# Another order for the start of a fused attention and gated-MLP kernel, with two attention visits and two weight steps moved

## The chip, the cores and the metric

One core of a Trainium2 chip runs the whole program. The time is that of one execution on the device, in microseconds (us). TensorE (PE in the profile) multiplies matrices, VectorE (DVE) and ScalarE (ACT) work on vectors, GpSimd (POOL) does elementwise work too, and the queues of SyncE (SP), ACT and POOL issue the transfers.

## The reference

```
scores = scale * np.matmul(q, k.transpose(0, 1, 3, 2))        # q, k, v: 8 x 8 heads x 576 x 64, fp32
masks = np.stack([mask_plain if h < H // 2 else mask_dil for h in range(H)])   # window 32, or 32 at every 4th key
attn = np.exp(scores - max); attn = attn / (sum + 1e-09)
x = (attn @ v).transpose(0, 2, 1, 3).reshape(B * S, H * D)    # 4608 tokens x 512
g = x @ w_gate                                                # 512 x 1536
out = (g * (1 / (1 + exp(-g))) * (x @ w_val)) @ w_out         # 1536 x 512
```

## The kernel before

**Tokens and packs.** The 4608 tokens are 12 chunks of 384. The attention of a chunk is four packs (two heads each), numbered on through the chunks. A pack's life is a row of steps: Q scores (L320 puts the mask, L326 the products), S subtracts the row maximum (L340, L341 on DVE), X is the exponential (L346 on ACT), T turns the exponentials on TensorE (L350), K copies them out of PSUM (L356 on ACT), A multiplies by the values (L366), N divides by the sums (L375 to L377 on DVE), U turns the result (L384), H and L make the two halves of x (L413 on ACT, L417 on DVE). Chunk 0's four packs are all worked at the start of the program; the later packs are worked between the matrix products of the MLP.

**Products in two halves.** Every fp32 operand is a sum of a high part, rounded to fp32r, and a low part, and a product is three matmuls: high x high, high x low, low x high. In the first four chunks a step s of `for s in range(NS)` is one block of 128 hidden columns: 12 matmuls for the gate (`gv_mm(ci, f, 0)`, bank bg, L428), 12 for the value (bank bv, L428), and 12 of the step before for the output (`out_mm`, banks bo, L465). Between them ACT makes the tanh (L437), DVE multiplies the gate in place (`dve_u`, L442) and the value (`dve_h`, L447), ACT and POOL split h in two halves (L452, L457). The gate's bank is single: the next gate products wait for L442.

**Weights.** They arrive as raw 64-bit words and each unit (half a block; block f has units 2f and 2f+1) goes through five steps, which the table of the start names W0 to W4: W0 the exponents (E, L207 on ACT), W1 a shift (T: L225 on ACT for units 1, 2 and odd ones from 5 on, else L228 on DVE), W2 the join of the two words (B: L235 or L238 on DVE), W3 the high half (H, L246 on ACT), W4 the low half (L, L250 on POOL). Every token `Wn` takes the next unit that has not had that step. A raw buffer is loaded again when step B of its unit is done.

**What sets the order.** During the start the list of tokens is the order in which TensorE, DVE and ACT get the instructions. After it a scheduler places the instructions; the program's calls (`w_upto`, `attend`) give it their order. `visits(m, a, b)` says in which of the slots (three to a step s) pack m's first visit A (scores of m, results of m-1) and second visit B (turning of both) are written.

Of the kernel before, what the change touches and what calls it, by code (L numbers as in the profile page):

```python
# [106 lines left out]
def attention_moe(ctx, tc, qkb, vb, w, masks, ident, out):  # L107
# [148 lines left out]
    def w_upto(**to):  # L256
        for c, n in to.items():
            while done[c] < min(n, NU):
                w_one(c)

    def w_one(c):
        u = done[c]
        done[c] += 1
        if c == "E":
            w_exp(u)
        elif c == "T":
            w_shift(u)
        elif c == "B":
            w_bits(u)
            while ready["w"] and w_load():  # L270
                pass
        elif c == "H":
            w_split_hi(u)
        else:
            w_split_lo(u)
# [145 lines left out]
    def gv_mm(ci, f, which):  # L421
        bank = (bank_g, bank_v)[which]
        xh, xl = x_hi[ci % 2], x_lo[ci % 2]

        ops = [(j, 0, x) for j in range(NK) for x in (xh, xl)] + [(j, 1, xh) for j in range(NK)]
        for n, (j, low, x) in enumerate(ops):
            o = 4 * P * (j // 2) + 2 * P * which + P * (j % 2)
            nc.tensor.matmul(out=bank[:, :CH], lhsT=wcol(f, o, low), rhs=x[ORDER[j]],  # L428
                             start=n == 0, stop=n == len(ops) - 1)
# [5 lines left out]
    def act_tanh(i):  # L435
        t = t_ring()
        nc.scalar.activation(out=t, in_=bank_g[:, :CH], func=AF.Tanh, scale=0.5)  # L437
        hst[i] = [t, None, None]

    def dve_u(i):  # L440
        t = hst[i][0]
        last["h"] = nc.vector.scalar_tensor_tensor(out=t, in0=t, scalar=1.0, in1=bank_g[:, :CH],  # L442
                                                   op0=ALU.add, op1=ALU.mult)

    def dve_h(i):
        t = hst[i][0]
        last["h"] = nc.vector.scalar_tensor_tensor(out=t, in0=t, scalar=0.5, in1=bank_v[:, :CH],  # L447
                                                   op0=ALU.mult, op1=ALU.mult)

    def h_hi(i):  # L450
        hh = hh_ring(dt=F32R)
        nc.scalar.copy(out=hh, in_=hst[i][0])  # L452
        hst[i][1] = hh

    def h_lo(i):
        hl = at(M_H + 4 * CH, CH, F32R)
        nc.gpsimd.tensor_tensor(out=hl, in0=hst[i][0], in1=hst[i][1], op=ALU.subtract)  # L457
        hst[i][2] = hl

    def out_mm(i):  # L460
        f = i % NF
        _, hh, hl = hst.pop(i)

        for j, low, x in [(j, low, hh) for j in range(4) for low in range(2)] + [(j, 0, hl) for j in range(4)]:
            nc.tensor.matmul(out=bank_o[j][:, :CH], lhsT=wcol(f, 2 * DM + P * j, low), rhs=x,  # L465
                             start=f == 0 and low == 0 and x is hh, stop=f == NF - 1 and x is hl)

    def out_store(ci):
        for j in range(4):
            ot = at(M_RAW + 8 * WU - CH * (j + 1), CH)  # L470
            if j % 2 == 0:
                nc.scalar.copy(out=ot, in_=bank_o[j][:, :CH])
            else:
                nc.vector.tensor_copy(out=ot, in_=bank_o[j][:, :CH])
            nc.sync.dma_start(out=out[P * j:P * j + P, CH * ci:CH * ci + CH], in_=ot)
# [47 lines left out]

    et = mybir.EngineType
    with tc.manual_schedule(engines={et.PE, et.DVE, et.Activation}):
        for what in ("Q0 Q1 S0 X0 T0 S1 K0 X1 A0 M0 W0 Q2 N0 T1 K1 S2 X2 Q3 W1 S3 X3 A1 U0 N1 W2 T2 K2 H0 L0 W0 W3 "
                     "W4 T3 A2 K3 W1 U1 N2 A3 H1 L1 W0 W2 U2 N3 W3 H2 U3 L2 W4 H3 L3 W1 W0 W2 W1 W2 W3 W0 W0").split():
            first[what[0]](int(what[1]))
    ab.close()
    bank_g, bank_v, two, *bank_o = [bank(ctx, *x) for x in (("bg", 1), ("bv", 1), ("two", 2), ("bo0", 1), ("bo1", 1),  # L530
# [13 lines left out]
    def visits(m, a, b):  # L544
        visit[a], visit[b] = ("A", m), ("B", m)
# [1 line left out]

    M1 = 4 * NPLAIN + 8
    for n in range(5):
        visits(4 + n, 5 + 13 * n // 2, 8 + 13 * n // 2)  # L550
    for m in range(9, M1 - 12):
        visits(m, NB * m // 4 - NB - 6, NB * m // 4 - NB - 2)
    for n in range(13):
# [8 lines left out]
    def attend(now):  # L562
        what, m = visit.get(now, ("", 0))
        if what == "A":
            if m > 4:
                results(m - 1, two)
            if m < NPK:
                scores(m, two, m < 8)
            if m > 4:
                norm(m - 1, two, later)  # L570
            if m < NPK:
                shift(m, two, later, m < 8)
                exps(m)

                with tc.issue_after(last["e"].ins):
                    load_v(m, later, nc.scalar)
                if m + 1 < NPK:
                    load_qk(m + 1, later, nc.scalar)
        elif what == "B":
            if m > 4:  # L580
                turn_y(m - 1, two[:, 0])
            if m < NPK:
                turn_e(m, two[:, 1])
                keys(m, two[:, 1], later)
            if m > 4:
                x_copies(m - 1, two[:, 0])
# [81 lines left out]
    def ask(n):  # L668

        nonlocal asked  # L670
        while asked < min(n, NPIECE * NC):
            taken[asked] = at(M_RING + PIECE * (asked % NAT), PIECE, F32R)
            nc.gpsimd.dma_start(out=taken[asked], in_=pieces[asked % NPIECE])  # L673
            asked += 1
# [31 lines left out]
    def x_step(n, ci):  # L706
        b11, b12, b21, b22 = [x32[a][t] for a in range(2) for t in range(2)]
        if ci == 0:
            b11, b21 = x32_first
        x1 = x1_at[min(ci, 1)]  # L710
        steps = [lambda: x_split(0, b11), lambda: x_split(1, b21), lambda: tt(nc.vector, x1, b12, b11),
                 lambda: x_split(3, x1), lambda: tt(nc.vector, x1, b22, x1), lambda: x_split(2, x1),
                 lambda: tt(nc.vector, b12, b22, b12), lambda: tt(nc.vector, b21, b21, x1),
                 lambda: x_split(4, b12), lambda: x_split(5, b21), lambda: x_split(6, b22)]
        if n < len(steps):
            steps[n]()
# [66 lines left out]
    def n_out(ci, t, i):  # L783
        return NT * NP * ci + NP * t + i
# [9 lines left out]
    def mix_to(half):  # L794

        while mixed < half * 9 * NP // 62:
            mix_stage()

    for s in range(NS):
        ci, f = divmod(s, NF)  # L800
        W = 2 * s
        w_upto(L=W + 3)
        gv_mm(ci, f, 0)
        act_tanh(s)
        w_upto(H=W + 4, E=W + 6)
        attend(3 * s)
        dve_u(s)
        mix_to(2 * (s - NF) + 1)
        with tc.issue_after(last["h"].ins):
            w_upto(T=W + 5, B=W + 5)  # L810
        w_upto(L=W + 4, H=W + 5, E=W + 7)
        gv_mm(ci, f, 1)
        attend(3 * s + 1)
        dve_h(s)
        h_hi(s)
        with tc.issue_after(last["h"].ins):
            w_upto(T=W + 6, B=W + 6)
        if s > 0:
            out_mm(s - 1)
        h_lo(s)  # L820
        if s > 0 and f == 0:
            out_store(ci - 1)
        attend(3 * s + 2)

        mix_to(2 * (s - NF) + 2)
        if ci == NPLAIN - 1:
            if f >= 9:
                ask([4, 7, NAT - 1][f - 9])
            for n in {5: (0,), 6: (1,), 7: (2,), 8: (3,), 9: (4, 5), 10: (6, 7, 8), 11: (9, 10)}.get(f, ()):
                x_step(n, 0)  # L830


    for ci in range(NC):
# [14 lines left out]
        for t in range(NT):  # L848
            for i in range(NP):
                n = n_out(ci, t, i)  # L850
# [60 lines left out]
```

## Time and profile before

| | us |
|---|---|
| median of 3 runs | 955.54 (955.46 to 956.37) |
| the profiled execution, its own time | 955.79 |
| its span, first to last instruction | 953.8 |

| engine | busy us | share of the span |
|---|---|---|
| TensorE matmul | 940.8 | 99% |
| TensorE weight load | 915.3 | 96% |
| DVE | 658.4 | 69% |
| ACT | 406.9 | 43% |
| POOL | 378.8 | 40% |

The busy share is a mean over the whole program. The change touches its first hundred us alone, so what counts is which engine waits there, and for what.

### The profile page before, as it was taken

To read this page: it belongs to the slowest core of one execution; us is meant where nothing else is said; L and a number is where in the kernel's file an instruction comes from. 1 tells how busy PE (TensorE), PEld (TensorE's weight loads), DVE (VectorE), ACT (ScalarE), POOL (GpSimd) and SP (SyncE) were. 2 spreads that over 40 slices of the span, in tenths; PEclk is the share of its full clock that TensorE was granted. 3 is DMA by queue.
4 is the path that set the end of the run, shared out by engine and by line. 5 is a ranking of instruction groups with operands and counts; after the bars stand their busy time and mean duration, and the time that the engine had idled before them with its cause. 6 is when DMAs were issued, how large, how long until landed. Compare 5 with 4: busy or idle time off the path is not lost.

```text
span 953.8 us, 23938 instructions
## 1 busy us (share of the span) xinstructions
PE 940.8 (99%) x9960; PEld 915.3 (96%) x9960; DVE 658.4 (69%) x1168; ACT 406.9 (43%) x788; POOL 378.8 (40%) x460
## 2 busy tenths in 40 slices
PE   7899999999999999999999999999999999999998
PEld 5898999999999999999999999999999999999998
DVE  4966557667767654776887677789487779466583
ACT  4885332333234323444554344446234446234352
POOL 0865421111112222344276334465244448354472
PEclk9999999999999999999999999999999999999999
DMA  9976154666766781989888998889988878988883
GB/s 367 344 260 202 35 205 160 228 208 220 241 231 224 253 308 56 288 262 297 269 263 278 339 288 259 264 251 298 350 264 283 254 236 267 317 250 255 252 238 121
DMA packets 86060, 238.12 MB, mean 250 GB/s; under 512 B 8768, under 2 KB 29120, under 8 KB 85952
## 3 DMA queue, kind: packets, MB, share of 16 engines
q0 software_dynamic: 36288, 132.14, 44.9%
q1 hardware_dynamic: 36848, 65.07, 19.5%
q10 hardware_dynamic: 12816, 39.38, 12.3%
q8 instruction: 79, 1.29, 0.6%
q14 instruction: 29, 0.24, 0.1%
HBM read 194.08 MB, written 42.47 MB: 248 GB/s over the span
## 4 chain that ended last, share of the span: by engine, by line
PE 89%; DVE 6%; ACT 3%; issue 1%; DMA 1%; POOL 0%; ACTq 0%; DVEq 0%; POOLq 0%; SPq 0%
PE bo L741 31%; PE bg L741 11%; PE bv L741 11%; PE bo L465 9%; PE bv L428 9%; PE bg L428 9%; PE two L366 3%; PE two L326 2%; PE two L350 2%; PE two L384 1%; DVE at_float32r L700 1%; DVE at_int L235 1%; ACT at_int L207 1%; DVE at_int L238 1%; ACT at_int L225 1%
## 5 line engine op out<-in xcount | busy, mean ns | idle before, releaser
L741 PE MATMUL bo<-at_float32r,at_float32r 128*128 128x384 f32 x1728 | 318.8, 336 | 0.0
L741 PEld LDWEIGHTS bo<-at_float32r,at_float32r 128*128 128x128 f32 x1728 | 299.9, 188 | 1.1
L673 POOL DMA_DIRECT2D at_float32r<-pieces x252 | 137.8, 547 | 245.5 <-PE bo L741 141.6
L700 DVE TENSOR_TENSOR at_float<-bo,at_float 128x384 f32<-128x384 f32 x224 | 122.3, 554 | 101.5 <-PE bo L741 51.9
L457 POOL TENSOR_TENSOR at_float32r<-at_float,at_float32r 128x384 fp32r<-128x384 f32 x48 | 57.3, 1193 | 215.7 <-PE bo L465 179.7
L741 PE MATMUL bg<-at_float32r,at_float32r 128*128 128x384 f32 x648 | 137.1, 337 | 0.0
L741 PE MATMUL bv<-at_float32r,at_float32r 128*128 128x384 f32 x648 | 136.6, 336 | 0.0
L741 PEld LDWEIGHTS bv<-at_float32r,at_float32r 128*128 128x128 f32 x648 | 114.2, 188 | 0.5
L741 PEld LDWEIGHTS bg<-at_float32r,at_float32r 128*128 128x128 f32 x648 | 113.8, 188 | 0.7
L700 DVE TENSOR_TENSOR at_float32r<-at_float,at_float32r 128x384 fp32r<-128x384 f32 (+1 forms) x112 | 101.5, 930 | 18.3 <-ACT at_float32r L730 14.3
L428 PE MATMUL bg<-at_float32r,at_float32r 128*128 128x384 f32 x576 | 111.6, 340 | 1.4 <-POOL at_float32r L250 0.8
L428 PE MATMUL bv<-at_float32r,at_float32r 128*128 128x384 f32 x576 | 111.3, 340 | 0.0
L730 ACT CAST at_float32r<-at_float 128x384 fp32r<-128x384 f32 x168 | 82.6, 512 | 65.2 <-PE bv L741 21.9
L465 PE MATMUL bo<-at_float32r,at_float32r 128*128 128x384 f32 x576 | 109.3, 337 | 0.0
L700 POOL TENSOR_TENSOR at_float32r<-at_float,at_float32r 128x384 fp32r<-128x384 f32 x84 | 91.6, 1091 | 43.9 <-ACT at_float32r L730 42.8
L428 PEld LDWEIGHTS bg<-at_float32r,at_float32r 128*128 128x128 f32 x576 | 100.4, 188 | 3.0 <-POOL at_float32r L250 1.1
L428 PEld LDWEIGHTS bv<-at_float32r,at_float32r 128*128 128x128 f32 x576 | 100.4, 188 | 0.9
L465 PEld LDWEIGHTS bo<-at_float32r,at_float32r 128*128 128x128 f32 x576 | 100.6, 188 | 0.4
L767 ACT ACTIVATE at_float<-at_float 128x384 f32<-128x384 f32 x96 | 50.6, 527 | 99.6 <-DVE at_float L700 99.6
L442 DVE SCALAR_TENSOR_TENSOR at_float<-at_float,bg 128x384 f32<-128x384 f32 x48 | 26.6, 553 | 73.3 <-ACT at_float L437 73.3
L746 ACT COPY at_float<-bg 128x384 f32<-128x384 f32 x84 | 40.3, 479 | 82.3 <-PE bg L741 82.1
L700 DVE TENSOR_TENSOR at_float<-at_float,at_float 128x384 f32<-128x384 f32 (+1 forms) x64 | 53.8, 865 | 24.5 <-POOL at_float32r L700 11.5
(80 smaller groups left out, 992.8 us busy)
## 6 DMA issues: line engine op xcount, KB each, us to landing
at_float32r<-pieces POOLq DMA_DIRECT2D x252, 512.0 KB, 4.7
pieces<-at_float32r SPq DMA_DIRECT2D x126, 256.0 KB, 3.5
at_int<-w SPq DMA_DIRECT2D x24, 768.0 KB, 6.5
at_float<-vb ACTq DMA_DIRECT2D x36, 390.0 KB, 4.8
out<-at_float SPq DMA_DIRECT2D x48, 192.0 KB, 4.2
at_float<-qkb ACTq DMA_DIRECT2D x14, 448.0 KB, 5.7
at_float<-qkb ACTq DMA_DIRECT2D x15, 400.0 KB, 5.5
at_float<-qkb ACTq DMA_DIRECT2D x7, 640.0 KB, 6.7
```

What stands on the lines that cost most here:

```text
L326: nc.tensor.matmul(out=two[BQ * j:BQ * j + BQ, h, a + BK * g:a + BK * g + BK], lhsT=t[r, q:q + BQ], rhs=t[r, k:k + BK], start=not masked, ...
L366: nc.tensor.matmul(out=two[BQ * j:BQ * j + BQ, h, (D + 1) * g:(D + 1) * (g + 1)], lhsT=t[r, BQ * i:BQ * i + BQ], rhs=v[r, i, :], start=Tru ...
L428: nc.tensor.matmul(out=bank[:, :CH], lhsT=wcol(f, o, low), rhs=x[ORDER[j]], start=n == 0, stop=n == len(ops) - 1)
L442: last["h"] = nc.vector.scalar_tensor_tensor(out=t, in0=t, scalar=1.0, in1=bank_g[:, :CH], op0=ALU.add, op1=ALU.mult)
L457: nc.gpsimd.tensor_tensor(out=hl, in0=hst[i][0], in1=hst[i][1], op=ALU.subtract)
L465: nc.tensor.matmul(out=bank_o[j][:, :CH], lhsT=wcol(f, 2 * DM + P * j, low), rhs=x, start=f == 0 and low == 0 and x is hh, stop=f == NF - ...
L673: nc.gpsimd.dma_start(out=taken[asked], in_=pieces[asked % NPIECE])
L700: engine.tensor_tensor(out=out, in0=a, in1=b, op=op)
L730: nc.scalar.copy(out=o[:, 0], in_=src)
L741: nc.tensor.matmul(out=bank, lhsT=w, rhs=x, start=first and n == 0 and t in FRESH, stop=last and n == len(ops) - 1, skip_group_check=True)
L746: nc.scalar.copy(out=kept[KEPT[t]][r], in_=banks[0][r][:, :CH])
L767: nc.scalar.activation(out=f, in_=g, func=AF.Tanh, scale=0.5)
```

## The change

There are three edits.

The table of the start is written in another order. Pack 1's turned exponentials (T1) now stand ahead of pack 2's scores (Q2); pack 1's results (A1) ahead of pack 3's scores; pack 3's turning (T3) behind pack 2's results (A2). Among the weights' steps, unit 0's shift (the first W1) stands ahead of pack 2's S, unit 1's exponents (the second W0) behind K3 and unit 0's high half, and unit 1's join (the second W2) behind N3.

The second visit of packs 4 and 5 is written one slot later. The exponents of units 22 and 23 (steps s of 8 and 9) are asked for half a step later.

```diff
-        for what in ("Q0 Q1 S0 X0 T0 S1 K0 X1 A0 M0 W0 Q2 N0 T1 K1 S2 X2 Q3 W1 S3 X3 A1 U0 N1 W2 T2 K2 H0 L0 W0 W3 "
-                     "W4 T3 A2 K3 W1 U1 N2 A3 H1 L1 W0 W2 U2 N3 W3 H2 U3 L2 W4 H3 L3 W1 W0 W2 W1 W2 W3 W0 W0").split():
+        for what in ("Q0 Q1 S0 X0 T0 S1 K0 X1 A0 M0 T1 N0 K1 W0 W1 Q2 S2 A1 X2 N1 Q3 T2 U0 S3 K2 H0 X3 W2 A2 L0 T3 "
+                     "N2 K3 W3 W4 W0 U1 W1 A3 H1 L1 N3 U2 W0 W2 H2 U3 L2 W3 H3 L3 W4 W1 W0 W2 W1 W2 W3 W0 W0").split():
             first[what[0]](int(what[1]))
...
     for n in range(5):
-        visits(4 + n, 5 + 13 * n // 2, 8 + 13 * n // 2)
+        visits(4 + n, 5 + 13 * n // 2, 8 + 13 * n // 2 + (n < 2))
...
-        w_upto(H=W + 4, E=W + 6)
+
+        w_upto(H=W + 4, E=W + 6 - (s == 9))
...
-        w_upto(L=W + 4, H=W + 5, E=W + 7)
+        w_upto(L=W + 4, H=W + 5, E=W + 7 - (s == 8))
```

ACT's queue before, from pack 2's exponentials on (in the names, at_1536_int_167, 173 and 269 are the raw words of units 0, 1 and 2, fk, fx and fs PSUM banks):

```order
L346 ACTIVATE at_384_float_230<-at_384_float_230 128x384
L346 ACTIVATE at_384_float_238<-at_384_float_238 128x384
L356 COPY at_384_float_241<-fk 128x384
L413 CAST at_384_float32r<-fx 128x384
L207 ACTIVATE at_1536_int_173<-at_1536_int_173 128x768
L246 CAST at_1536_float32r<-at_776_int_337 128x768
L356 COPY at_384_float_306<-fs_123 128x384
L225 ACTIVATE at_1536_int_173<-at_1536_int_173 128x768
```

The same place of ACT's queue in the changed program:

```order
L346 ACTIVATE at_384_float_230<-at_384_float_230 128x384
L356 COPY at_384_float_241<-fk 128x384
L413 CAST at_384_float32r<-fx 128x384
L346 ACTIVATE at_384_float_238<-at_384_float_238 128x384
L356 COPY at_384_float_279<-fs_123 128x384
L246 CAST at_1536_float32r<-at_776_int_282 128x768
L207 ACTIVATE at_1536_int_173<-at_1536_int_173 128x768
L225 ACTIVATE at_1536_int_173<-at_1536_int_173 128x768
```

Unit 1's exponents (L207) moved from ahead of unit 0's high half (L246) and K3 (L356 out of fs_123) to behind both.

DVE's queue before, from pack 1's low half of x on (fr is the bank of the results):

```order
L417 TENSOR_TENSOR at_384_float32r<-fx,at_384_float32r 128x384
L235 SCALAR_TENSOR_TENSOR at_776_int_419<-at_1536_int_173 128x3x256
L375 TENSOR_SCALAR at_6_float_369<-fr 128x6
L376 RECIPROCAL at_6_float_369<-at_6_float_369 128x6
L377 TENSOR_TENSOR at_384_float_370<-fr,at_6_float_369 128x2x3x64
```

The same place in the changed program:

```order
L417 TENSOR_TENSOR at_384_float32r<-fx,at_384_float32r 128x384
L375 TENSOR_SCALAR at_6_float_337<-fr 128x6
L376 RECIPROCAL at_6_float_337<-at_6_float_337 128x6
L377 TENSOR_TENSOR at_384_float_338<-fr,at_6_float_337 128x2x3x64
L235 SCALAR_TENSOR_TENSOR at_776_int_425<-at_1536_int_173 128x3x256
```

Unit 1's join (L235) moved behind pack 3's division.

TensorE's queue before, from pack 0's last turning (U0) on:

```order
L384 MATMUL fx<-at_256_float_59,at_384_float_299 128x128 x3
L350 MATMUL fk<-at_256_float_59,at_384_float_230 128x128 x3
L350 MATMUL fs_123<-at_256_float_59,at_384_float_238 128x128 x3
L366 MATMUL fr<-at_780_float_171,at_384_float_241 32x65 x24
L384 MATMUL fx<-at_256_float_59,at_384_float_370 128x128 x3
```

The same five groups in the changed program:

```order
L350 MATMUL fk<-at_256_float_59,at_384_float_230 128x128 x3
L384 MATMUL fx<-at_256_float_59,at_384_float_275 128x128 x3
L366 MATMUL fr<-at_780_float_171,at_384_float_241 32x65 x24
L350 MATMUL fs_123<-at_256_float_59,at_384_float_238 128x128 x3
L384 MATMUL fx<-at_256_float_59,at_384_float_338 128x128 x3
```

T3 (L350 into fs_123) moved from ahead of A2 (L366) to behind it, and T2 (L350 into fk) from behind U0 (the first L384) to ahead of it. With the third edit alone the instructions stand, on every engine, in the order of the program before; and with all three no engine's order differs behind the first 568 TensorE instructions of the program, the first 68 of DVE and the first 80 of ACT.

## Rows read from the trace of the kernel before

**Rows 1.** Windows: microseconds, busy time and count by engine, PEclk, DMA share, GB/s.
```profile
0.00:33.50 33.50, 26.20 (x489) 20.37 (x490) 19.77 (x37) 19.71 (x32) 8.88 (x9) 1.00 0.94 353
33.50:110.00 76.50, 74.35 (x890) 70.66 (x889) 53.32 (x75) 51.34 (x79) 51.77 (x31) 1.00 0.64 222
110.00:940.00 830.00, 829.93 (x8527) 814.24 (x8526) 582.55 (x1052) 335.37 (x679) 317.53 (x421) 1.00 0.79 251
```
**Rows 2.** Waits of TensorE, 0 to 130 us: total us, times, longest.
```profile
PE two L384 <- DVE at_float L341: 1.2, 1, 1.2
PE fs L326 <- issue: 1.0, 1, 1.0
...
PE two L350 <- ACT at_float L346: 0.9, 1, 0.9
PE bg L428 <- POOL at_float32r L250: 0.8, 1, 0.8
```
**Rows 3.** Timeline of TensorE: start us, length us, operation, count, [idle before, releaser].
```profile
13.12 0.42 PE L326 MATMUL fs<-at_float 64*32 64x64 f32 x3 [1.02 <-issue]
...
16.88 0.84 PE L350 MATMUL fk<-at_float,at_float 128*128 128x128 f32 x3
...
18.29 0.46 PE L366 MATMUL fr<-at_float,at_float 64*32 64x65 f32 x14
19.39 0.51 PE L366 MATMUL fr<-at_float,at_float 64*32 64x65 f32 x34 [0.64 <-issue]
19.83 0.55 PE L384 MATMUL fx<-at_float,at_float 128*128 128x128 f32 x3
...
30.80 0.96 PE L428 MATMUL bg<-at_float32r,at_float32r 128*128 128x384 f32 x4 [0.77 <-POOL at_float32r L250]
31.61 2.27 PE L428 MATMUL bv<-at_float32r,at_float32r 128*128 128x384 f32 x12
...
35.82 2.24 PE L428 MATMUL bg<-at_float32r,at_float32r 128*128 128x384 f32 x12
```
**Rows 4.** Timeline of ACT, 14 to 25 us.
```profile
14.84 0.53 ACT L346 ACTIVATE at_float<-at_float 128x384 f32<-128x384 f32 x1
...
17.75 0.48 ACT L356 COPY at_float<-fk 128x384 f32<-128x384 f32 x1 [0.35 <-PE fk L350]
...
18.50 0.91 ACT L207 ACTIVATE at_int<-at_int 128x768 f32<-128x768 f32 x1
19.29 0.84 ACT L246 CAST at_float32r<-at_int 128x768 fp32r<-128x768 f32 x1
20.01 0.50 ACT L356 COPY at_float<-fs 128x384 f32<-128x384 f32 x1
...
23.16 0.83 ACT L246 CAST at_float32r<-at_int 128x768 fp32r<-128x768 f32 x1 [0.67 <-DVE at_int L235]
```
**Rows 5.** Timeline of DVE, 14 to 46 us.
```profile
14.72 0.94 DVE L228 TENSOR_SCALAR at_int<-at_int 128x768 int32<-128x768 int32 x1
...
23.05 0.16 DVE L375 TENSOR_SCALAR at_float<-fr 128x6 f32<-128x6 f32 x1
...
23.46 0.56 DVE L377 TENSOR_TENSOR at_float<-fr,at_float 128x384 f32<-128x384 f32 x1
...
28.18 0.95 DVE L238 SCALAR_TENSOR_TENSOR at_int<-at_int,at_int 128x768 int32<-128x768 int32 x1
...
32.12 1.87 DVE L235 SCALAR_TENSOR_TENSOR at_int<-at_int 128x768 int32<-128x768 int32 x1 [0.56 <-ACT at_int L225]
33.96 0.55 DVE L442 SCALAR_TENSOR_TENSOR at_float<-at_float,bg 128x384 f32<-128x384 f32 x1
...
45.62 0.68 DVE L340 TENSOR_REDUCE at_float<-two 128x8 f32<-128x512 f32 x1
```
**Rows 6.** Timeline of POOL, 24 to 35 us.
```profile
24.07 1.74 POOL L250 TENSOR_TENSOR at_float32r<-at_int,at_float32r 128x768 fp32r<-128x768 f32 x1 [2.13 <-ACT at_float32r L246]
28.31 4.87 POOL L250 TENSOR_TENSOR at_float32r<-at_int,at_float32r 128x768 fp32r<-128x768 f32 x2 [2.49 <-ACT at_float32r L246]
33.13 1.75 POOL L457 TENSOR_TENSOR at_float32r<-at_float,at_float32r 128x384 fp32r<-128x384 f32 x1
```

## Prediction

> **What bounds the kernel now.** I read the windows first. From 110 to 940 us TensorE is busy 829.93 of 830.00 us; from 33.5 to 110 it lacks 76.50 - 74.35 = 2.15 us, and before 33.5 it lacks 7.30 [rows 1]. So the end is TensorE's own work laid behind whatever delay its first 110 us collect: a microsecond lost there is a microsecond on the whole, and nothing later gives it back, since no wait stands there to absorb it. The change reorders only that stretch.
>
> Next, TensorE's waits there: a pause of 1.0 in which it waited for nothing the profile shows (issue, inside Q2), 0.8 for a low half from POOL, 0.9 at pack 4's second visit for ACT and 1.2 at a later one for DVE [rows 2]. The 0.8 ends at 30.80, and from 35.82 a whole set of 12 matmuls follows the last [rows 3]. So three landmarks carry the argument: 30.80 (unit 2's low half), the end of the value products that begin at 31.61, and 35.82 (gate products of s = 2). Last, the timelines of ACT, DVE and POOL ahead of them, to see what makes the weight units come when they do.
>
> **The change, part by part.**
>
> *Third edit (exponents of units 22 and 23).* By itself it leaves the order of all engines as it was, and so does nothing: 0. The 1.2 us wait [rows 2] at about 93 us, in whose neighbourhood those exponents stand, therefore stays.
>
> *T1 in front of Q2.* T1 is three transposes of some 0.84 [rows 3]. The pause of 1.02 stands in Q2; if it is a fixed moment, T1 lies in it and costs nothing, and everything on TensorE behind it gains 0.84; if it comes after a fixed number of instructions, T1 only changes places. But the packs are not what 23 to 36 us wait for, so I follow what the gain meets.
>
> *When K3 runs.* ACT's K3 stood at 20.01 [rows 4]. In the new order it waits for T3, which stands behind A2, behind K2, behind T2, behind X2. X2 ran at 14.84 [rows 4]; unit 0's shift (0.94, [rows 5]) is now ahead of pack 2's maximum on DVE. I let half of it show: X2 at 15.3, done at 15.85. T2 0.84: 16.7. K2 0.48 [rows 4]: 17.2. A2 took 0.46 + 0.51 [rows 3]: 18.15. T3 0.84: 19.0. A2 also held a pause of 0.64 [rows 3], and of what stood ahead of it only T3 has left: with it, 19.6. So K3 at 19.0 to 19.6, and I take 19.6: the packs gain 0.4.
>
> *Unit 1's high half.* Before, it followed K3 by 23.16 - 20.01 = 3.15 [rows 4]; between them stood unit 1's L225, pack 1's two halves of x and unit 1's join. Now three more things stand between: unit 0's high half (start to next start 20.01 - 19.29 = 0.72) and unit 1's exponents (19.29 - 18.50 = 0.79), both [rows 4], and on DVE pack 3's division (23.05 to 23.46 + 0.56, 0.97 [rows 5]). So it begins at 19.6 + 3.15 + 0.72 + 0.79 + 0.97 = 25.2 instead of 23.16: 2.1 later. Those instructions ran on ACT before while K3 was not yet there; now ACT stands idle for K3 and DVE for pack 1's x. That is the heart of the forecast.
>
> *Through POOL to TensorE.* Unit 1's low half began 0.91 behind its high half and took 1.74 [rows 6]: now 26.1 to 27.85. The rows show that L235 and L238 never run beside a POOL subtraction: L235 is listed from 32.12 to 33.99, more than its usual 0.95, while POOL's second L250 ends at 33.18 [rows 5, 6]. So unit 2's join, ready at about 27 (its L225 follows unit 1's high half and one x copy on ACT), waits to 27.85 and ends 0.85 later, 28.7; its high half follows (0.75), and POOL starts unit 2's low half at 29.5. Before, that one was held from 28.31 to 29.13 by an L238 (28.18 + 0.95) and ended at 30.77; now that L238 comes second, and the low half ends at 29.5 + 1.64 = 31.15: only 0.4 late. But the L238 of unit 3 runs then, to 32.05, unit 3's high half to 32.85, and its low half from 32.9 to 34.55, where it ended at 28.31 + 4.87 = 33.18: 1.37 late [rows 6]. The last four value products of s = 1 need it; they began at 31.61 + 8 x 0.175 = 33.0, where 0.175 is (35.82 - 31.61) / 24 matmuls [rows 3]: just covered. So TensorE now waits 1.37.
>
> Then the gate products of s = 2 need L442, which stood on DVE behind two joins. Unit 4's join must wait for POOL to 34.55 and ends at 35.4; POOL's L457, waiting since, takes its turn (33.13 + 1.75 - 33.99 = 0.89 alone [rows 5, 6]) to 36.3; unit 5's join ends at 37.2 and L442 (0.55) at 37.75, where it ended at 34.51 [rows 5]. TensorE would come at 35.82 + 1.37 = 37.2 and waits to 37.8: 0.6 more. Hence 2.0 on TensorE.
>
> [...]
>
> *Bounds.* With K3 at 19.0 and L457 behind unit 5's join: 0.8. With K3 at its old 20.01: 2.4.
>
> *Second edit (visits).* Pack 4's turning (L350) stands one matmul earlier among the value products, not later. Its 0.9 wait [rows 2] is for the chain maximum, subtraction, exponential; the maximum (L340, 0.68 [rows 5]) now runs ahead of a join, the subtraction still behind it. So up to 0.68 could go; but DVE had 35.82 - 34.51 = 1.31 in hand at s = 2 [rows 3, 5] and now has none, which costs up to 1.31 - 0.68 = 0.63. Between -0.68 and +0.63 I take +0.4, since the join stays in the chain. Pack 5's turning moves behind 12 matmuls (2.24, [rows 3]) and its division of x behind a shift of 0.94 [rows 5]; its results are asked for a whole step later, so 0, at worst 0.94.
>
> **Sum.** 2.0 + 0.4 = 2.4. The profiled execution took 955.79 (span 953.8, 2.0 around it), 0.25 over the median of 955.54; on the median the forecast is 957.9. From the bounds: 0.8 - 0.68 = +0.1 to 2.4 + 0.63 + 0.94 = +4.0, so 955.6 to 959.5.
>
> **The rivals.**
>
> [...]
>
> [...]
>
> *Faster.* The gain at the front (0.84) reaches 30.80 whole, because TensorE rather than ACT sets the first 25 us, and pack 4's wait of 0.9 goes: 955.54 - 1.7 = 953.8. It decides if unit 1's high half begins before 23.16. Against it: ACT's new order puts it behind K3 by 5.6, so K3 would have to run before 17.5, when X3 is hardly done.
>
> **Chances.** Forecast 0.66; swallowed, or the clock, 0.24; faster 0.10. Less than 0.2% (1.9 us) is about what a measurement of this kernel cannot tell from no change. Of the forecast's share 0.62 lies above 957.4; of the faster one 0.06 below 953.6. So slower 0.63, same 0.31, faster 0.06. The likeliest case alone spans 956.6 to 959.5; to hold 8 in 10 the range goes down to 954.8 and ends at 959.5.
>
> **What would show it.** In the changed profile: unit 1's L246 at about 25 instead of 23.16, with ACT idle before K3 and before that L246 (for DVE's L235); unit 3's low half ending near 34.5; TensorE's waits near 33 and 37 for POOL and DVE; gate products of s = 2 near 38. Wrong if K3 comes before 18.5, if the gate products of s = 2 start before 36.5, or if something behind 110 us differs.

## The result, and the profile after

The changed kernel takes 958.95 us (median of 5 runs, 957.84 to 960.44), the kernel before 955.46 (955.05 to 956.37): ratio 1.0039, 95% interval 1.0028 to 1.0051, slower by 3.5 us. The profiled execution took 958.95, with a span of 956.9 where it was 953.8. In the comparison for e12 below, one run of the kernel before that took 1300.48 at a granted clock of 0.658 is left out.

Windows of the changed kernel, columns as in [rows 1]:

```profile
0.00:33.50 33.50, 26.49 (x474) 20.87 (x474) 16.81 (x35) 16.41 (x27) 5.45 (x7) 1.00 0.84 317
33.50:110.00 76.50, 74.08 (x885) 70.16 (x886) 55.37 (x76) 53.58 (x82) 55.06 (x33) 1.00 0.69 237
110.00:940.00 830.00, 829.93 (x8527) 814.23 (x8526) 578.53 (x1050) 334.02 (x675) 317.69 (x420) 1.00 0.78 251
```

Behind 110 us nothing has changed: 829.93 of 830 as before. In the first 33.5 us TensorE is even busier than before (26.49 against 26.20), yet it has started 15 matmuls fewer (474 against 489): the same work takes it longer. Up to 110 us its idle time is the same (9.43 against 9.45), yet 20 matmuls fewer have started; so the loss doesn't show in TensorE's idle time. POOL has done 5.45 us instead of 8.88.

TensorE's waits in the first 130 us (total, times, longest), to be laid beside [rows 2]:

```profile
PE fr L366 <- issue: 1.9, 1, 1.9
PE two L384 <- DVE at_float L341: 1.3, 2, 1.1
...
PE bg L428 <- POOL at_float32r L250: 0.7, 1, 0.7
PE bv L428 <- ACT at_float32r L246: 0.7, 1, 0.7
...
PE fs L326 <- issue: 0.5, 1, 0.5
...
PE two L350 <- ACT at_float L346: 0.3, 1, 0.3
```

The first pause, inside Q2, went from 1.0 to 0.5, but the second, inside A2 (L366), from 0.64 to 1.9. Pack 4's wait (L350) fell from 0.9 to 0.3. TensorE's timeline shows where the A2 pause stands and what lies behind it:

```profile
17.04 0.53 PE L366 MATMUL fr<-at_float,at_float 64*32 64x65 f32 x17
19.50 0.69 PE L366 MATMUL fr<-at_float,at_float 64*32 64x65 f32 x31 [1.94 <-issue]
20.12 0.90 PE L350 MATMUL fs<-at_float,at_float 128*128 128x128 f32 x3
...
25.24 1.80 PE L428 MATMUL bg<-at_float32r,at_float32r 128*128 128x384 f32 x5
...
27.16 0.84 PE L384 MATMUL fs<-at_float,at_float 128*128 128x128 f32 x3
...
29.32 1.04 PE L428 MATMUL bg<-at_float32r,at_float32r 128*128 128x384 f32 x5
...
34.18 0.97 PE L428 MATMUL bg<-at_float32r,at_float32r 128*128 128x384 f32 x4 [0.74 <-POOL at_float32r L250]
...
39.18 2.25 PE L428 MATMUL bg<-at_float32r,at_float32r 128*128 128x384 f32 x12
```

The pause ends at 19.50; before, it ended at 19.39 [rows 3], although TensorE had come to it 1.2 us later then. T3 (L350), which before lay in front of it, now stands behind it. Five gate products take 1.80 at 25.24 and 1.04 at 29.32, and three transposes still take 0.84 at 27.16 where they took 0.55 at 19.83 [rows 3]: by these durations the lower clock level lasts until behind 27, where it had ended by 19.8 (the packed trace's first record of the granted clock reads 1.00 from 28.70 on; before, from 18.96 on). The two landmarks of the prediction are 3.38 and 3.36 late (34.18 for 30.80, 39.18 for 35.82).

ACT from K3 on, beside [rows 4]:

```profile
21.11 0.48 ACT L356 COPY at_float<-fs 128x384 f32<-128x384 f32 x1 [3.12 <-PE fs L350]
21.49 0.83 ACT L246 CAST at_float32r<-at_int 128x768 fp32r<-128x768 f32 x1
22.22 0.91 ACT L207 ACTIVATE at_int<-at_int 128x768 f32<-128x768 f32 x1
...
26.66 0.84 ACT L246 CAST at_float32r<-at_int 128x768 fp32r<-128x768 f32 x1 [1.22 <-DVE at_int L235]
28.04 0.48 ACT L413 CAST at_float32r<-fs 128x384 fp32r<-128x384 f32 x1 [0.54 <-PE fs L384]
28.41 0.91 ACT L225 ACTIVATE at_int<-at_int 128x768 int32<-128x768 uint32 x1
```

ACT stands idle for 3.12 in front of K3, which waits for T3, and unit 1's high half (26.66) comes 5.55 behind K3. DVE, beside [rows 5]:

```profile
25.20 0.56 DVE L377 TENSOR_TENSOR at_float<-fr,at_float 128x384 f32<-128x384 f32 x1
25.68 0.95 DVE L235 SCALAR_TENSOR_TENSOR at_int<-at_int 128x768 int32<-128x768 int32 x1
...
31.55 0.95 DVE L238 SCALAR_TENSOR_TENSOR at_int<-at_int,at_int 128x768 int32<-128x768 int32 x1
...
46.56 0.68 DVE L340 TENSOR_REDUCE at_float<-two 128x8 f32<-128x512 f32 x1
47.16 1.91 DVE L235 SCALAR_TENSOR_TENSOR at_int<-at_int 128x768 int32<-128x768 int32 x1
```

POOL, beside [rows 6]:

```profile
31.74 4.81 POOL L250 TENSOR_TENSOR at_float32r<-at_int,at_float32r 128x768 fp32r<-128x768 f32 x2 [2.43 <-ACT at_float32r L246]
```

Unit 1's join (L235) now follows pack 3's division (L377). L238 begins ahead of POOL's pair of low halves again, by 0.19 (31.55 for 31.74), as it did by 0.13 before: the turn fell the same way, 3.4 later.

### The profile page after: what moved, and what is told of

It is laid out like the page before. It is cut to its first block, busy times and chain, and to the rows that moved or that the text cites. A ratio compares the mean times of both kernels' runs of the same rounds, so it can differ in the third digit from the quotient of the medians.

```text
span 956.9 us, 23938 instructions
## 1 busy us (share of the span) xinstructions
PE 944.0 (99%) x9960; PEld 918.4 (96%) x9960; DVE 655.0 (68%) x1168; ACT 406.9 (43%) x788; POOL 380.2 (40%) x460
## 4 chain that ended last, share of the span: by engine, by line
PE 92%; DVE 4%; ACT 2%; issue 1%; DMA 1%; ACTq 0%; DVEq 0%; SPq 0%
PE bo L741 31%; PE bg L741 11%; PE bv L741 11%; PE bo L465 10%; PE bg L428 10%; PE bv L428 10%; PE two L366 3%; PE two L326 2%; PE two L350 2%; PE two L384 2%; DVE at_float32r L700 1%; DVE at_int L235 1%; DVE at_float L700 0%; DMA at_int<-w 0%; DMA at_bfloat<-masks 0%
## 5 line engine op out<-in xcount | busy, mean ns | idle before, releaser
L700 DVE TENSOR_TENSOR at_float32r<-at_float,at_float32r 128x384 fp32r<-128x384 f32 (+1 forms) x112 | 98.8, 904 | 21.1 <-ACT at_float32r L730 17.2
L442 DVE SCALAR_TENSOR_TENSOR at_float<-at_float,bg 128x384 f32<-128x384 f32 x48 | 26.6, 553 | 74.2 <-ACT at_float L437 74.2
```

The costliest lines, as they stand in the source:

```text
L700: engine.tensor_tensor(out=out, in0=a, in1=b, op=op)
```

## The experiments

Two theories stood against each other. **A**, the prediction's: unit 1's steps, put behind K3 and N3, make TensorE late. **B**: TensorE's second pause ends at a moment that its own work doesn't move; what is put behind it (T3) is late, and the clock stays low. The differences below are to the kernel before on the same chip. The last column is from each profile: from TensorE's restart behind the second pause to its gate products of s = 2. It leaves out that the whole start lies some tenths earlier in one execution than in another. Some profiles are of executions off the median: e5's took 955.69 and e7's 957.90, the fastest of their kernels.

| kernel | median, us | difference | ratio, 95% interval | restart to s = 2, us |
|---|---|---|---|---|
| before | 955.46 | | | 35.82 - 19.39 = 16.4 |
| changed | 958.95 | +3.5 | 1.0028 to 1.0051 | 19.7 |
| e1 table alone | 958.47 | +3.1 | 1.0023 to 1.0050 | 19.1 |
| e2 visits alone | 956.33 | +0.9 | 1.0003 to 1.0021 | 16.3 |
| e3 changed, unit 1 ahead | 957.41 | +2.0 | 1.0011 to 1.0029 | 17.4 |
| e4 before, unit 1 late | 957.59 | +2.2 | 1.0011 to 1.0029 | 17.6 |
| e5 changed, T3 ahead | 957.49 | +2.6 | 1.0017 to 1.0038 | 17.6 |
| e6 before, T1 in front | 954.74 | -0.1 | 0.9989 to 1.0006 | 16.1 |
| e7 changed, 6 matmuls more | 959.51 | +4.7 | 1.0034 to 1.0059 | 19.1 |
| e8 before, pack 5's visit | 955.37 | +0.5 | 0.9997 to 1.0015 | 16.2 |
| e9 changed, 4 in the pause | 961.53 | +6.6 | 1.0061 to 1.0086 | 22.4 |
| e10 changed, join ahead | 958.62 | +3.7 | 1.0028 to 1.0053 | 19.1 |
| e11 before, pack 4's scores | 954.59 | -0.4 | 0.9988 to 1.0005 | 16.4 |
| e12 before, T3 behind A2 | 956.52 | +0.8 | 0.9996 to 1.0014 | 17.9 |

**e1 and e2, the two edits apart.** e1 has the new table and the old visits and exponents; e2 is the line of the visits alone:

```diff
-        visits(4 + n, 5 + 13 * n // 2, 8 + 13 * n // 2)
+        visits(4 + n, 5 + 13 * n // 2, 8 + 13 * n // 2 + (n < 2))
```

> The table of the start alone in its new order; visits and exponents as before. Both theories put the loss in the first 30 us, so both expect about the changed kernel's time, 958.5 to 959.5. If the two visits carry a part of it, this run lies below that by their share.

> The second visits of packs 4 and 5 a slot later, everything else as before. The prediction's term for them was +0.4, between -0.68 and +0.63 for pack 4 and up to +0.94 for pack 5: 955.9, at most 957.1. If pack 4's wait of 0.9 shrinks to 0.3 here as in the changed kernel, the edit itself made it shrink and the time falls to about 954.9; if the wait stays at 0.9, it shrank there only because all around it came later.

The table makes 3.1 of the 3.5; the rest is within the intervals. The visits alone cost 0.9 (interval 0.3 to 2.0). In e2 pack 4's wait stays at 0.90, and in e1 it is 0.35, so the table is what shrank it in the changed kernel, not the visits. In e2 there is also a new wait, when pack 6 comes to be turned (timeline of TensorE, e2):

```profile
76.65 0.55 PE L384 MATMUL two<-at_float,at_float 128*128 128x128 f32 x3 [0.57 <-DVE at_float L341]
```

**e8, pack 5's visit alone** (the edit of e2 with `n == 1`).

> The kernel before with only pack 5's second visit a slot later (pack 4's stays). The two together cost 0.9 and showed a new wait of 0.57 at 76.6, where pack 6 is turned. If that is pack 5's doing, its wait is here too and the time is 956.0 to 956.4; if pack 4's, 955.3 to 955.6.

The new wait is here as well (TensorE's waits from 52 to 110 us, where e1 has one of 1.0):

```profile
PE two L384 <- DVE at_float L341: 1.6, 2, 1.0
```

So it is pack 5's turning, put later, that makes pack 6's late. In the changed kernel that wait is only 0.20. In e8 the time moves by 0.5, which its interval doesn't tell from nothing.

**e3 and e4, unit 1's steps undone, and done alone.** In e3 the changed table gets unit 1's exponents ahead of K3 and its join ahead of N3 again:

```diff
-        for what in ("Q0 Q1 S0 X0 T0 S1 K0 X1 A0 M0 T1 N0 K1 W0 W1 Q2 S2 A1 X2 N1 Q3 T2 U0 S3 K2 H0 X3 W2 A2 L0 T3 "
-                     "N2 K3 W3 W4 W0 U1 W1 A3 H1 L1 N3 U2 W0 W2 H2 U3 L2 W3 H3 L3 W4 W1 W0 W2 W1 W2 W3 W0 W0").split():
+        for what in ("Q0 Q1 S0 X0 T0 S1 K0 X1 A0 M0 T1 N0 K1 W0 W1 Q2 S2 A1 X2 N1 Q3 T2 U0 S3 K2 H0 X3 W0 W2 A2 L0 "
+                     "T3 N2 W3 W4 K3 W1 U1 A3 H1 L1 W0 W2 U2 N3 W3 H2 U3 L2 W4 H3 L3 W1 W0 W2 W1 W2 W3 W0 W0").split():
```

In e4 the table before gets them behind:

```diff
-        for what in ("Q0 Q1 S0 X0 T0 S1 K0 X1 A0 M0 W0 Q2 N0 T1 K1 S2 X2 Q3 W1 S3 X3 A1 U0 N1 W2 T2 K2 H0 L0 W0 W3 "
-                     "W4 T3 A2 K3 W1 U1 N2 A3 H1 L1 W0 W2 U2 N3 W3 H2 U3 L2 W4 H3 L3 W1 W0 W2 W1 W2 W3 W0 W0").split():
+        for what in ("Q0 Q1 S0 X0 T0 S1 K0 X1 A0 M0 W0 Q2 N0 T1 K1 S2 X2 Q3 W1 S3 X3 A1 U0 N1 W2 T2 K2 H0 L0 T3 A2 "
+                     "K3 W3 W4 W0 U1 W1 N2 A3 H1 L1 N3 U2 W0 W2 H2 U3 L2 W3 H3 L3 W4 W1 W0 W2 W1 W2 W3 W0 W0").split():
```

> The changed kernel with unit 1's exponents again ahead of K3 and of unit 0's high half, and its join again ahead of N3; TensorE's order is the changed one. Theory A (the order of unit 1's steps made the loss, as predicted): its high half no longer hangs on K3, begins near 23.2, the gate products of s = 2 begin at 36 to 36.5, time 955.5 to 956.5. Theory B (the second pause of 1.94 and the lower clock level up to 28.7 made it): pause and clock stay, pack 0 to 3 end as late as in the changed kernel, gate products of s = 2 at 38.5 or later, 957.5 to 959.

> The kernel before with only unit 1's exponents put behind K3 and its join behind N3; TensorE's first 24 us keep their old order, so pause (0.64) and clock (rise near 19) stay as before. Theory A: K3 at 18.6 to 19, unit 1's high half 5.6 behind it at about 24.4, 1.2 late, time 956.5 to 957.5. Theory B: the loss came with the pause and the clock, which are untouched here: 955.3 to 956.

Neither theory is enough. With unit 1 ahead, 2.0 are left; with unit 1 late alone, 2.2 come. TensorE's timeline in e3, the restart and the gate products of s = 2:

```profile
19.32 0.68 PE L366 MATMUL fr<-at_float,at_float 64*32 64x65 f32 x31 [0.86 <-issue]
...
36.72 2.25 PE L428 MATMUL bg<-at_float32r,at_float32r 128*128 128x384 f32 x12
```

ACT's in e3, unit 1's high half:

```profile
24.07 0.83 ACT L246 CAST at_float32r<-at_int 128x768 fp32r<-128x768 f32 x1 [0.66 <-DVE at_int L235]
```

The high half is 2.59 earlier than in the changed kernel but still 0.91 behind 23.16 [rows 4], and s = 2 is 0.90 late with it. e4 brings out something else: its high half begins at 23.78, only 0.62 late, and yet s = 2 is 1.17 late. POOL's timeline in e4:

```profile
24.69 1.76 POOL L250 TENSOR_TENSOR at_float32r<-at_int,at_float32r 128x768 fp32r<-128x768 f32 x1 [3.47 <-ACT at_float32r L246]
28.20 1.76 POOL L250 TENSOR_TENSOR at_float32r<-at_int,at_float32r 128x768 fp32r<-128x768 f32 x1 [1.76 <-ACT at_float32r L246]
31.72 1.76 POOL L250 TENSOR_TENSOR at_float32r<-at_int,at_float32r 128x768 fp32r<-128x768 f32 x1 [1.76 <-ACT at_float32r L246]
```

DVE's in e4:

```profile
28.51 2.27 DVE L238 SCALAR_TENSOR_TENSOR at_int<-at_int,at_int 128x768 int32<-128x768 int32 x1
```

TensorE's in e4:

```profile
36.99 2.36 PE L428 MATMUL bg<-at_float32r,at_float32r 128*128 128x384 f32 x12 [0.73 <-DVE at_float L442]
...
49.69 0.66 PE L350 MATMUL two<-at_float,at_float 128*128 128x128 f32 x4 [1.71 <-ACT at_float L346]
```

Here POOL and DVE take turns: each low half waits 1.76 for a high half, whose join had waited for the low half before it, so a unit comes every 3.51. On ACT the tanh of s = 1 stands behind such a high half and begins at 35.88; L442 waits for it, and TensorE 0.73 for L442. Pack 4 waits 1.71. The join at 28.51 is listed with 2.27 instead of 0.95 and ends 0.82 behind the subtraction of 28.20, as if most of its own time came only behind that. POOL's idle 1.76 is such a join's own time and the high half behind it. What makes the two engines wait for each other, no run shows.

**e5, T3 ahead of A2 again, in the changed kernel.** On TensorE only T3 moves (and one value product past A3); the other engines keep their order.

```diff
-        for what in ("Q0 Q1 S0 X0 T0 S1 K0 X1 A0 M0 T1 N0 K1 W0 W1 Q2 S2 A1 X2 N1 Q3 T2 U0 S3 K2 H0 X3 W2 A2 L0 T3 "
+        for what in ("Q0 Q1 S0 X0 T0 S1 K0 X1 A0 M0 T1 N0 K1 W0 W1 Q2 S2 A1 X2 N1 Q3 T2 U0 S3 K2 H0 X3 W2 T3 A2 L0 "
```

> The changed kernel with T3 put ahead of A2 again, so that it stands in front of TensorE's second pause; unit 1's steps stay behind K3. Theory B (the pause ends at 19.3 to 19.5 whatever stands before it, so what lies behind it sets K3): the idle part of the pause shrinks from 1.9 to under 1.0, K3 goes from 21.1 to 18.8 to 19.3, unit 1's high half from 26.7 to 24.4 to 24.9, time 956.7 to 957.7, as with unit 1 late alone. Theory C (the pause is a fixed length behind a fixed instruction, or only the clock counts): K3 no earlier than 20.3, time 958.3 or more.

TensorE's timeline in e5:

```profile
17.03 0.55 PE L350 MATMUL fs<-at_float,at_float 128*128 128x128 f32 x3 [1.10 <-ACT at_float L346]
...
19.16 0.75 PE L366 MATMUL fr<-at_float,at_float 64*32 64x65 f32 x33 [1.32 <-issue]
```

ACT's in e5:

```profile
17.67 0.48 ACT L356 COPY at_float<-fs 128x384 f32<-128x384 f32 x1 [0.69 <-PE fs L350]
...
24.21 0.83 ACT L246 CAST at_float32r<-at_int 128x768 fp32r<-128x768 f32 x1 [0.57 <-DVE at_int L235]
```

K3 is 3.4 earlier, even more than B expected, and against C, which had it no earlier than 20.3; the pause still ends at 19.16, after 1.32 idle. The high half gains only 2.45: its join stands behind N3, N3 waits 0.48 for A3 on DVE (its L375 at 22.33), and A3 stands behind the pause. The median of 957.49 lies in B's 956.7 to 957.7, but it is 2.6 over the kernel before on this chip, with an interval that reaches from 1.6 to 3.6: K3, not the time, decides against C. The gain on the changed kernel, 0.9, comes from two comparisons on different chips and is only rough.

**e12, T3 behind A2 alone, in the kernel before.** No other instruction of any engine moves.

```diff
-                     "W4 T3 A2 K3 W1 U1 N2 A3 H1 L1 W0 W2 U2 N3 W3 H2 U3 L2 W4 H3 L3 W1 W0 W2 W1 W2 W3 W0 W0").split():
+                     "W4 A2 T3 K3 W1 U1 N2 A3 H1 L1 W0 W2 U2 N3 W3 H2 U3 L2 W4 H3 L3 W1 W0 W2 W1 W2 W3 W0 W0").split():
```

> The kernel before with only T3 put behind A2; TensorE's order alone changes. Theory B: the second pause still ends at 19.1 to 19.5, T3 now lies behind it with the rest of A2, so K3 comes at 20.3 to 20.9 instead of 20.0, unit 1's high half 3.1 behind it, and everything to the gate products of s = 2 goes with it: 0.3 to 0.9 over the kernel before; if the clock then stays at its lower level beyond 22, 1 to 1.5 over it. Theory A (only unit 1's own steps matter, 20.0 was set by ACT's queue and not by T3): K3 stays within 0.2 of where it was and the time within 0.3.

TensorE's timeline in e12:

```profile
18.91 0.69 PE L366 MATMUL fr<-at_float,at_float 64*32 64x65 f32 x31 [0.59 <-issue]
19.53 0.90 PE L350 MATMUL fs<-at_float,at_float 128*128 128x128 f32 x3
```

ACT's in e12:

```profile
20.52 0.48 ACT L356 COPY at_float<-fs 128x384 f32<-128x384 f32 x1 [0.90 <-PE fs L350]
...
23.65 0.83 ACT L246 CAST at_float32r<-at_int 128x768 fp32r<-128x768 f32 x1 [0.65 <-DVE at_int L235]
```

From the restart to K3 it is now 1.61, where it was 20.01 - 19.39 = 0.62 [rows 3, 4], and from K3 to the high half 3.13 as before (3.15). From the restart to s = 2 the move costs 1.5 in this execution, a part of it perhaps through the clock: T3 took 0.90 at 19.53 here, and in [rows 3] three transposes took 0.55 at 19.83. Both pauses of this execution ended half a microsecond early, so less of it shows in the clock time of s = 2 (36.81, 0.99 late). The median is 0.8 up, and the interval, from -0.4 to 1.3, doesn't tell that from nothing; K3's place is what the run shows.

**e6, T1 in front of Q2 alone.**

```diff
-        for what in ("Q0 Q1 S0 X0 T0 S1 K0 X1 A0 M0 W0 Q2 N0 T1 K1 S2 X2 Q3 W1 S3 X3 A1 U0 N1 W2 T2 K2 H0 L0 W0 W3 "
+        for what in ("Q0 Q1 S0 X0 T0 S1 K0 X1 A0 M0 W0 T1 N0 K1 Q2 S2 X2 Q3 W1 S3 X3 A1 U0 N1 W2 T2 K2 H0 L0 W0 W3 "
```

> The kernel before with T1, N0 and K1 in front of Q2 and nothing else moved. Theory B: both pauses end where they did (13.1 and 19.4), T1's 0.84 only makes the second one longer, and what counts behind 19.4 stays: 955.0 to 956.0; more only if the clock rises later than 19 (up to 1.5 more). Theory C (the pauses hang on the number of instructions, T1 changes places with Q2): packs 1 to 3 as before or up to 0.8 earlier, 954.6 to 955.5, and the second pause keeps its 0.6.

Nothing moves (-0.1). The first pause shrinks from 1.02 to 0.55 idle; what T1 filled there comes back as a wait of 0.40 in front of T3 and in the second pause, 0.87 for 0.64 (TensorE, e6):

```profile
18.99 0.51 PE L366 MATMUL fr<-at_float,at_float 64*32 64x65 f32 x34 [0.87 <-issue]
```

**e10, the join ahead of N3, in the changed kernel.**

```diff
-                     "N2 K3 W3 W4 W0 U1 W1 A3 H1 L1 N3 U2 W0 W2 H2 U3 L2 W3 H3 L3 W4 W1 W0 W2 W1 W2 W3 W0 W0").split():
+                     "N2 K3 W3 W4 W0 U1 W1 A3 H1 L1 W2 N3 U2 W0 H2 U3 L2 W3 H3 L3 W4 W1 W0 W2 W1 W2 W3 W0 W0").split():
```

> The changed kernel with only unit 1's join ahead of N3 again; its exponents stay behind K3 and unit 0's high half. The chain of the prediction has 0.97 for N3 out of the 5.6 behind K3. By it unit 1's high half comes 0.9 to 1.0 earlier (25.7), the gate products of s = 2 at 38.2, and the time is 2.3 to 2.8 over the kernel before. If N3 is no link of the chain (pack 3's own lateness or POOL's order sets unit 2), 3.2 or more over the kernel before.

ACT's timeline in e10:

```profile
25.81 0.83 ACT L246 CAST at_float32r<-at_int 128x768 fp32r<-128x768 f32 x1 [0.32 <-DVE at_int L235]
```

DVE's in e10:

```profile
46.03 2.51 DVE L235 SCALAR_TENSOR_TENSOR at_int<-at_int 128x768 int32<-128x768 int32 x1
48.46 0.68 DVE L340 TENSOR_REDUCE at_float<-two 128x8 f32<-128x512 f32 x1
```

TensorE's in e10:

```profile
50.58 0.66 PE L350 MATMUL two<-at_float,at_float 128*128 128x128 f32 x4 [1.07 <-ACT at_float L346]
```

The link is there: the high half comes 0.85 earlier (25.81 for 26.66), s = 2 0.53. The time, 3.7 over the kernel before, is still not the 2.3 to 2.8 that the link alone would give: ACT waits 0.86 instead of 0.54 for pack 3's turning, and more is given back at pack 4: DVE's join L235 stands ahead of the maximum L340 again, and TensorE's wait is 1.07 instead of 0.33. So the order of these two on DVE decides that wait, 0.74 of it, in a kernel whose early stage is nearly the changed one's.

**e11, pack 4's scores a slot earlier, in the kernel before** (`5 + 13 * n // 2 - (n == 0)`).

> The kernel before with pack 4's first visit (its scores) one slot earlier, the second where it was. Its turning waited 0.9 for the chain of maximum, subtraction and exponential; with a slot more between the visits that wait goes: 0.5 to 0.9 under the kernel before. If the scores then wait for their operands, or DVE is no earlier at the maximum, 0 to 0.5 over it.

The scheduler gave every engine the same order as before, so this tells nothing of the slot; pack 4's wait stays (0.93). It is the order of before once more: -0.4, interval -1.1 to +0.5.

**e7 and e9, the clock.** In e7 six small matmuls stand behind U1; in e9 four of 128x512 between U0 and A2. In e9 they are written over pack 2's turned exponentials before K2 copies these, so that pack 2's results are changed and K2 waits for the four. The edit of e7,

```diff
+    def fill():
+        for _ in range(6):
+            nc.tensor.matmul(out=bank_k[:, :P], lhsT=warm, rhs=warm, start=True, stop=True)
+        "F": lambda n: fill(),
-                     "N2 K3 W3 W4 W0 U1 W1 A3 H1 L1 N3 U2 W0 W2 H2 U3 L2 W3 H3 L3 W4 W1 W0 W2 W1 W2 W3 W0 W0").split():
+                     "N2 K3 W3 W4 W0 U1 F0 W1 A3 H1 L1 N3 U2 W0 W2 H2 U3 L2 W3 H3 L3 W4 W1 W0 W2 W1 W2 W3 W0 W0").split():
```

and in e9:

```diff
+    def fill():
+        for _ in range(4):
+            nc.tensor.matmul(out=bank_k, lhsT=ident16, rhs=consts[:, :512], start=True, stop=True)
-        for what in ("Q0 Q1 S0 X0 T0 S1 K0 X1 A0 M0 T1 N0 K1 W0 W1 Q2 S2 A1 X2 N1 Q3 T2 U0 S3 K2 H0 X3 W2 A2 L0 T3 "
-                     "N2 K3 W3 W4 W0 U1 W1 A3 H1 L1 N3 U2 W0 W2 H2 U3 L2 W3 H3 L3 W4 W1 W0 W2 W1 W2 W3 W0 W0").split():
+        for what in ("Q0 Q1 S0 X0 T0 S1 K0 X1 A0 M0 T1 N0 K1 W0 W1 Q2 S2 A1 X2 N1 Q3 T2 U0 F0 S3 K2 H0 X3 W2 A2 L0 "
+                     "T3 N2 K3 W3 W4 W0 U1 W1 A3 H1 L1 N3 U2 W0 W2 H2 U3 L2 W3 H3 L3 W4 W1 W0 W2 W1 W2 W3 W0 W0").split():
```

> The changed kernel with six matmuls more (128 columns of bf16, result unused) in the 0.71 that TensorE waits behind U1, at 21.7 to 22.4; nothing else is moved. If the lower clock level from 19.5 to 28.7 carries a part of the loss, and unbroken work is what ends it, the rise comes at 23 to 25.5 and the time falls by 0.5 to 1.5: 957.4 to 958.4. If unit 1 alone sets what follows, the rise changes nothing that waits: 958.5 to 959.2. If the six stand in the way: up to 0.4 over the changed kernel.

> The changed kernel with four matmuls more (128x512 of bf16, result unused) between U0 and A2, in the time that TensorE is idle in its second pause. (With them the one value product that stood ahead of A3 is placed behind it.) Theory B (pause ends at a fixed moment): the idle part shrinks from 1.9 to about 0.3 to 0.6 and the pause still ends at 19.3 to 19.7, so the four cost nothing. If idle time in the pause is what keeps the clock at its lower level behind it, the rise comes before 22 and the time falls to 1.5 to 2.8 over the kernel before; if the clock goes by something else, rise at 24 or later and 3 to 4 over the kernel before.

Both missed. In e7 transposes take 0.84 as late as 26.80: the six raised nothing. In e9 the level was high before the four came (three transposes took 0.55 at 15.58) and stayed so, K3 came 0.9 earlier than in the changed kernel, and it was the slowest of all. One value product went behind A3, and what follows stands in another order: output products stand ahead of the gate's and wait 1.5 for ACT and 1.4 for POOL, and POOL takes turns with DVE as in e4. So e9 doesn't say what the level is worth, only that a higher one doesn't save this order.

## Why the prediction came out as it did

The sign, the place and the range were right: slower, all of it made before 110 us, 958.95 within 954.8 to 959.5. The point, 957.9, was 1.05 too low, and the sum came together otherwise than written: that the range held was in part luck. Of the signs, ACT's idle time in front of K3 and the wait for DVE's join came; unit 3's low half ended at 36.55 instead of 34.5, and the waits near 33 and 37 didn't come as described.

**When K3 runs: the step that failed.** The prediction took the second pause for a length ("A2 also held a pause of 0.64 ... with it, 19.6"). It is an end: 19.50 in the changed kernel, 19.39 before. What the moves of T1 and T3 took away in front of it went into 1.94 of idle time (e6 for T1), and T3, put from before the pause to behind it, was late: 1.61 from the restart to K3 instead of 0.62, as in e12. K3 came at 21.11, 1.5 later than forecast.

**Unit 1's high half.** The chain of 5.63 behind K3 measured 5.55, and e10 shows its link N3 (0.85, forecast 0.97). With K3 wrong, the high half came at 26.66 instead of 25.2: 3.50 late, 1.10 of it K3's own lateness and 2.40 the longer chain behind it (5.55 for 3.15). That unit 1's order has a price of its own, e3 and e4 show: about 1.5 to 2.2.

**Through POOL to TensorE.** The lateness of 3.5 went on whole (3.38, then 3.36), instead of shrinking from 2.1 to 0.4 and growing to 2.0. That forecast and trace both lose only 0.1 from one end of this leg to the other is luck. Unit 2's join didn't meet unit 1's subtraction, since unit 2's shift (28.41) came only behind pack 3's x, which waited for its own turning at 27.16; after that L238 began ahead of POOL's pair as before (by 0.19, then 0.13). The forecast's taking of turns and its extra wait for L442 do exist, but in e4, where it is 0.73 and comes through ACT's tanh, not through joins on DVE.

**T1 and the exponents.** T1 at nothing: e6 agrees. Of the prediction's two cases for the pause, a fixed moment and a fixed number of instructions, both held: the place is fixed by the number, the end by something else (last section). Of the exponents no run has them alone; that they move no instruction on any engine is as it was said, and the changed trace shows no new wait where they stand.

**The visits.** +0.4 in all was about the right size (the changed kernel's difference less e1's: 0.4; alone: 0.9; neither is told apart from the other) for the wrong reason. Pack 4's wait fell by 0.55 instead of costing 0.4: the maximum ahead of the join is worth it, and the new table brought that, not the visit (e1, e2, e10). Pack 5's move, taken at 0 with 0.94 as its worst, brought the wait at pack 6: 0.57 in e2, 0.20 in the changed kernel.

**The rivals.** Swallowed (little of the delay in the time) and faster are out. The clock counts as a loss: in the changed kernel the higher level came some ten us later than before (28.70 for 18.96). With T1 alone in front it came at about 17.5, an estimate from e6's windows (PEclk 0.50 from 13 to 17 us, 0.94 from 17 to 21), and the time didn't move (-0.1). The clock is not the whole loss: in e4 the level was high by 17.45, where T3 took 0.55, and 2.2 are lost. With the order of before the price is small: in e11 three transposes still took 0.90 at 19.88, where they took 0.55 in [rows 3], and from the restart to s = 2 it is 16.44 against 16.43. In the changed order a part can be read off. e1 has that order up to s = 2 and had the higher level right behind the restart (TensorE and ACT, e1):

```profile
19.67 0.55 PE L350 MATMUL fs<-at_float,at_float 128*128 128x128 f32 x3
20.31 0.48 ACT L356 COPY at_float<-fs 128x384 f32<-128x384 f32 x1 [2.51 <-PE fs L350]
```

K3 came 1.03 behind the restart there instead of 1.61, and from K3 to s = 2 it is 18.06 against 18.07 in the changed kernel: in these two executions the lower level behind the restart cost 0.58, and all of it arrives. Further on, five gate products lose 1.80 - 1.04 = 0.76 in front of pack 3's turning; ACT's idle 0.54 at 28.04 bounds what that can have made late on ACT.

By single edits the loss adds up roughly: T1 -0.1, T3 +0.8, unit 1 +2.2, visits +0.9, together 3.8 for 3.5. Each has some 0.9 of uncertainty either way.

No variant beat the kernel before by more than can be measured.

## What to carry to other kernels

When an engine's idle time is put down to nothing that the profile shows, find out from a second trace whether its place, its end or its length is fixed. Here the end was: work in front of it was free (T1), and work that came to stand behind it was late by its own length, with all that hung on it (T3). A step moved behind another on one queue inherits all that the other waits for; here unit 1 was made to hang on pack 3, and pack 3 on the pause. Where instructions of two engines hold each other back, look at who begins first in each variant: with L238 0.19 ahead of the subtraction two subtractions ran in 4.81 (changed kernel), with L238 0.31 behind it one came every 3.51 (e4).

## What the runs showed of the hardware that was not expected

**Pauses with a place and an end of their own.** In thirteen of the fourteen traces both pauses can be seen (in e9 the first can't). Whatever was moved, they stand at the same count: 222 matmuls lie in front of the first and 349 in front of the second (350 in e5's records), with 127 matmuls and 127 weight loads from one to the other (the kernel before and the changed one). The first ends between 12.6 and 13.4, the second 6.0 to 6.4 behind it, whether TensorE had idled 0.59 or 1.95 in it. The kernel before and the changed one each have two packets of 16,384 bytes on the queue that the profile calls "instruction" in that stretch (the kernel before, DMA queues from 10 to 18 us):

```profile
q8 instruction: 2, 0.03, 1.7%
```

They start at 10.71 and 16.99 there, at 10.59 and 17.02 in the changed kernel, and in both kernels each pause ends 2.4 to 2.6 behind the start of its packet (at 13.12 and 19.39; at 13.15 and 19.50). That TensorE waits there for what these packets bring is the author's reading of the times; no run moved a packet on purpose, so it is not shown, and what sets a packet's start was not tried.

**The clock's level in the start.** In e1 three transposes took 0.55 at 19.67 and 0.90 again at 23.09, behind the 1.90 of idle time in its second pause. Windows of e1, with PEclk as the third column from the right:

```profile
17.00:21.00 4.00, 1.64 (x54) 1.17 (x49) 1.88 (x5) 1.49 (x4) 0.00 (x0) 0.93 1.01 412
21.00:25.00 4.00, 3.43 (x56) 2.93 (x57) 1.42 (x5) 3.66 (x6) 1.74 (x1) 0.50 0.91 371
```

Windows of the changed kernel over the same stretch:

```profile
21.00:25.00 4.00, 3.29 (x58) 2.38 (x57) 0.92 (x4) 3.89 (x7) 1.75 (x1) 1.00 0.96 393
```

Here the column reads 1.00, though its three transposes at 23.90 took 0.90 too. This trace has no record of the clock before the one at 28.70, so for this stretch the durations of equal instructions count here, not the column. In e1 the level fell behind those 1.90 of idle time; that the idle time was the cause, no run here shows.
